# Linear attention and a routed mixture of experts on one core: seven raw and eleven split weight buffers instead of eleven and nine, splits six steps ahead instead of five, and small table columns kept in PSUM

## The chip, the cores and the metric

The kernel runs on one core of a Trainium2 chip. The metric is the device time of one execution in microseconds (us). Before the change it is 616.91 us (median of 3 runs, 615.19 to 617.08).

A core has five engines that run their own instruction streams in order and meet through semaphores: TensorE (PE, matmuls; its weight loads are listed as PEld), VectorE (DVE), ScalarE (ACT), GpSimd (POOL) and SyncE (SP, which issues most DMAs). SBUF is the large on-chip memory, PSUM the small one that matmuls write.

## The reference

```python
# attention: 8 batches, 8 heads, 576 rows, head size 64, 128 features
proj = einsum('bhsd,df->bhsf', x, w_phi)
proj = proj - max(abs(proj), axis=-1)
phi  = concatenate([exp(proj), exp(-proj)])
kv   = einsum('bhsf,bhsd->bhfd', phi(k), v);  z = sum(phi(k), axis=2)
attn = einsum('bhsf,bhfd->bhsd', phi(q), kv) / (phi(q) . z + 1e-6)

# experts: x is attn as (4608 rows, 512); 8 experts, hidden size 1024
do_compute = x @ w_skip > 0
e_idx  = argmax(x @ w_gate, axis=1);  gate_w = softmax(x @ w_gate) at e_idx
y      = gate_w * (relu(x @ w1[e_idx]) @ w2[e_idx])
out    = x + y where do_compute, else x
```

A row goes through one expert, the one with the highest gate, and rows with a skip score of zero or less go through none. All results are float32.

## The kernel before

**Two stages.** The first 337 us compute the attention, batch by batch, and the gate of each row; rows go to a table in DRAM (`xrows`) and to the output. The second stage runs the experts, and the change touches this stage alone.

**Expert slots and steps.** The rows of an expert are gathered into slots of 256 rows (kinds E and D), 192 rows (C) or 128 rows (S). The slots run in a fixed order, E E E C C (S with C) C (D with S) C D, numbered by kind: E0, E1, E2, C0, C1, S0, C2, C3, D0, S1, C4, D1. The weights of a slot are read in eight chunks of 512 KB, four of `w1` and four of `w2`. One chunk is one **step**; there are 96, numbered k = 0 to 95. E0 has steps 0 to 7, E1 8 to 15, E2 16 to 23, C0 24 to 31, C1 32 to 39. S0 and C2 share 40 to 55: S0's `w1` 40 to 43, half of C2's `w1` 44 and 45, S0's `w2` 46 to 49, the rest of C2's `w1` 50 and 51, C2's `w2` 52 to 55.

**What a step needs.** `fetch` (line 175) issues the load of chunk k on SP's queue into a raw buffer `wraw_c` (lines 184 and 187): *load k*. `split` (line 190) makes two tensors of it for matmuls at fp32 accuracy: ACT copies the chunk, rounded, to `hi` (line 195), then DVE (one instruction of 1024 columns) or POOL (four of 256 columns) subtracts it from the raw one to give `lo` (line 200): *split k*. Both halves lie in one of the pair buffers `w`. PE multiplies by `hi` and `lo`: `mm1` (lines 919, 922, 932, 933, 935) and `mm2` (946 to 951) for E, C and D, `half1` (848 to 850) and `half2` (869 to 871) for S.

**Buffers.** From chunk 12 on there are eleven raw buffers and nine pair buffers. A raw buffer is free for load k + 11 when split k is done; a pair buffer is free when PE is through step k.

**The order.** From line 1177 on, the order on each engine is the order in the code. A planner (lines 1144 to 1151) makes a time `T[k]` for each step and `parted[k]` for each split, from fixed costs. At the start of step k the loop (line 1203) emits the splits of up to five steps ahead, as far as the planner thinks that they can be done by then, and with split k also load k + 11. Then come PE's matmuls of step k, then extra work that is due at this step: gathers of rows (line 213, DMAs that POOL issues), the transposes `x` of gathered rows (lines 806 to 810), the stores of a finished slot (DVE `o` and `si`, lines 893 to 905, then a scatter that POOL issues, line 879), and pieces of `tables`.

**The tables.** `tables` (line 966) runs on DVE during steps 5 to 20. It works out from the counts of rows which rows go to which slot: per 128-row tile and expert it makes `tm`, reduces it to columns of 36 values (`pe`, `cc`, line 1029 and 1034), combines these in short instructions (`rk`, `lt`, `col`, lines 1030 to 1041), and compares `col` with a row of numbers (`eq`, line 1061) for PE, which sums up the indices in PSUM bank K.

Of the kernel before, what the change touches and what calls it, by code (L numbers as in the profile page):

```python
# [18 lines left out]
P = 128  # L19
# [5 lines left out]
def kernel(  # L25
# [23 lines left out]
    NT = NTOK // P  # L49
# [67 lines left out]
    eid0 = const.tile([1, 3], I32, name="eid0")  # L117
    idg0 = const.tile([P, 3, 2], I32, name="idg0")
    pad0 = const.tile([P, 3, 2], I32, name="pad0")
    const.tile([1, 40], I32, name="spare")  # L120
    mark = const.tile([1, 32], I32, name="mark")[:, 0:1]

    ft = const.tile([P, NSL, 4], I32, name="ft")
# [51 lines left out]
    def fetch(which, wap, c):  # L175
        i = nchunk[0]

        j = i % 4 if i < 12 else (i - 8) % 11
        rawp = wpool[0 if j < 4 else 3]
        nchunk[0] += 1  # L180
        raw = rawp.tile([P, 1024], F32, tag="wraw%d" % j, name="wraw_c", bufs=1)
        if which == 1:
            src = wap[:, :, c * FC:(c + 1) * FC].rearrange("o (k p) f -> p (o k) f", p=P)
            nc.sync.dma_start(out=raw.rearrange("p (k f) -> p k f", f=FC), in_=src)
        else:
            src = wap[:, c * FC:(c + 1) * FC, :].rearrange("o (k p) m -> p (o k) m", p=P)
            nc.sync.dma_start(out=raw.rearrange("p (k m) -> p k m", m=DM), in_=src)
        return which, i, raw

    def split(chunk, eng):  # L190
        which, i, raw = chunk
        s = i % 9
        pair = wpool[1 if s < 4 else 2].tile([P, 2, 1024], F32R, tag="w%d" % s, name="w", bufs=1)
        hi, lo = pair[:, 0], pair[:, 1]
        nc.scalar.activation(out=hi, in_=raw, func=AF.Copy)  # L195

        n = 256 if eng is nc.gpsimd else 1024
        for a in range(0, 1024, n):
            r = slice(a, a + n)
            eng.tensor_tensor(out=lo[:, r], in0=raw[:, r], in1=hi[:, r].bitcast(F32), op=ALU.subtract)  # L200
        w = FC if which == 1 else DM
        return hi.rearrange("p (k f) -> p k f", f=w), lo.rearrange("p (k f) -> p k f", f=w)
# [761 lines left out]
    start = {"E": 0, "D": 0, "C": NSD, "S": NS2}  # L964

    def tables():
        cn = bank("K")[:, 0:E]
        nc.tensor.matmul(cn, ones_b, Stot, start=True, stop=True)
        yield
        ni = const.tile([P, E], I32, name="ni")  # L970
# [40 lines left out]
        nc.vector.tensor_tensor(out=cf[:, 2], in0=cf[:, 2], in1=cf[:, 1], op=ALU.subtract)  # L1011

        rk = const.tile([P, NT], F32, name="rk")
        pe = const.tile([P, NT], F32, name="pe")
        tm = const.tile([P, NT, E], F32, name="tm")
        cc = const.tile([P, 3, NT], F32, name="cc")
        col = const.tile([P, NT], F32, name="col")
        lt = const.tile([P, NT], F32, name="lt")
        pk = const.tile([P, E], F32, name="pk")

# [8 lines left out]
        nc.vector.tensor_reduce(out=pe, in_=tm, axis=AX.X, op=ALU.add)  # L1029
        nc.vector.scalar_tensor_tensor(out=rk, in0=pe, scalar=-2.0, in1=RKH, op0=ALU.mult, op1=ALU.add)  # L1030
        yield
        for c in range(3):
            nc.vector.tensor_tensor(out=tm, in0=OH, in1=per_e(cf[:, c], NT), op=ALU.mult)
            nc.vector.tensor_reduce(out=cc[:, c], in_=tm, axis=AX.X, op=ALU.add)
        yield
        nc.vector.tensor_tensor(out=lt, in0=rk, in1=cc[:, 1], op=ALU.is_lt)
        nc.vector.tensor_tensor(out=col, in0=cc[:, 0], in1=cc[:, 2], op=ALU.subtract)
        nc.vector.tensor_tensor(out=col, in0=col, in1=lt, op=ALU.mult)
# [153 lines left out]
    with tc.manual_schedule():  # L1192
# [4 lines left out]
        for k, (w, x, c) in enumerate(steps):  # L1197
# [96 lines left out]
```

## Time and profile before

| | before |
|---|---|
| median of 3 runs | 616.91 us |
| profiled execution | 617.51 us |
| its span, first to last instruction | 615.8 us |
| mean granted TensorE clock | 0.984 |
| PE busy over the span | 571.6 us (93%) |
| DVE / ACT / POOL busy | 509.9 / 331.0 / 381.5 us |
| loads of weight chunks | 96 of 512 KB, 5.2 us median from issue to landing |

The time of an execution is its span and some 1.7 us around it. A row of the profile names the line, the engine, the operation and the tiles as out<-in. In the view in order of time (the timeline) a row begins with its start and its duration in us, several instructions of one kind in a row are one row with a count, and the bracket at its end is the engine's idle time ahead of it and who ended it. The list of waits sums such idle times up: total us, how many, the longest. The table by stretches gives each engine's busy time with its count of instructions, the granted clock as a share of full speed, the DMA engines' busy share and GB/s.

### The profile page before, as it was taken

The numbers are of one execution on the slowest core, as the hardware profiler recorded it, in microseconds if no ns is written. First come the engines' busy times: TensorE is split into PE (matmuls) and PEld (weight loads), VectorE is DVE, ScalarE is ACT, GpSimd is POOL, SyncE is SP. The second block draws the span as 40 slices with busy tenths as digits, with TensorE's granted clock in tenths as the row PEclk, the third lists the DMA queues.
The fourth block names the chain that finished last, engine by engine and source line by source line (L and its number), as shares of the span: only waits on it lengthen the run. The fifth ranks groups of instructions, "written<-read, shape, count | busy, mean of one in ns | idle before, by whom it ended". The sixth has DMA issues, their size and how long they took to land. (4 is left out here: it accounts for less than half of the span.)

```text
span 615.8 us, 18780 instructions
## 1 busy us (share of the span) xinstructions
PE 571.6 (93%) x7486; PEld 467.4 (76%) x7486; DVE 509.9 (83%) x1081; ACT 331.0 (54%) x649; POOL 381.5 (62%) x415
## 2 busy tenths in 40 slices
PE   4899999999999999998899799789999799999993
PEld 2577777767777677776667789588889589989892
DVE  5899999999989999999997679967688877956851
ACT  3465556556655555655544454334658556666620
POOL 5665585494855967667754756855467983559121
PEclk9899999999999999999999899999999899999997
DMA  9998888987677766423153499577686599597200
GB/s 157 160 157 150 186 184 178 196 184 142 134 162 160 160 114 155 119 73 113 37 160 127 136 338 341 170 275 228 216 263 203 178 297 327 175 318 238 76 19 30
DMA packets 250234, 108.34 MB, mean 176 GB/s; under 512 B 192417, under 2 KB 235553, under 8 KB 250144
## 3 DMA queue, kind: packets, MB, share of 16 engines
q1 hardware_dynamic: 245632, 97.58, 60.7%
q0 software_dynamic: 3200, 9.45, 4.5%
q8 instruction: 60, 0.98, 0.7%
q10 hardware_dynamic: 1312, 0.08, 0.1%
q14 instruction: 30, 0.25, 0.1%
HBM read 83.86 MB, written 24.02 MB: 175 GB/s over the span
## 5 line engine op out<-in xcount | busy, mean ns | idle before, releaser
L200 POOL TENSOR_TENSOR w<-wraw_c,w 128x256 fp32r<-128x256 f32 x124 | 109.8, 920 | 42.1 <-ACT w L195 36.0
L380 POOL TENSOR_TENSOR z<-ek 128x512 f32<-128x512 f32 x64 | 81.2, 1273 | 77.0 <-ACT ek L373 54.1
L195 ACT ACTIVATE w<-wraw_c 128x1024 fp32r<-128x1024 f32 x96 | 97.6, 1052 | 3.8 <-DMA wraw_c<-in_moe_w_dram 3.5
L200 DVE TENSOR_TENSOR w<-wraw_c,w 128x1024 fp32r<-128x1024 f32 x65 | 87.8, 1359 | 13.9 <-ACT w L195 12.8
L354 DVE TENSOR_REDUCE m<-ps_P 128x8 f32<-128x1024 f32 (+2 forms) x86 | 88.6, 1030 | 7.1 <-PE ps_P L347 7.1
L357 DVE TENSOR_TENSOR u<-ps_P,m 128x1024 f32<-128x1024 f32 (+2 forms) x86 | 88.8, 1033 | 2.9
L347 PE MATMUL ps_P<-wsrc,xT 64*64 64x128 f32 x2048 | 79.3, 283 | 11.7 <-DMA raw<-in_k_dram 7.1
L513 PEld LDWEIGHTS ps_O<-kva,eq 128*64 128x64 f32 x2048 | 74.0, 136 | 16.3 <-issue 5.8
L513 PE MATMUL ps_O<-kva,eq 128*64 128x74 f32 x2048 | 77.4, 228 | 3.8 <-DVE lgm L476 3.7
L347 PEld LDWEIGHTS ps_P<-wsrc,xT 64*64 64x64 f32 x2048 | 57.4, 135 | 28.2 <-issue 20.3
L399 ACT ACTIVATE eq<-ps_U 128x512 f32<-128x512 f32 x64 | 37.9, 593 | 64.7 <-PE ps_U L393 64.2
L415 PE MATMUL ps_K<-ek,v 128*64 128x256 f32 x512 | 72.0, 400 | 0.0
L879 POOL DMA_INDIRECT out_dram<-o,si x22 | 28.8, 1309 | 66.8 <-DVE si L878 60.4
L946 PE MATMUL ps_O<-w,hh 128*128 128x512 f32 x160 | 64.1, 401 | 0.0
L633 POOL TENSOR_SCALAR OP<-iota_p,rkp,wcol 128x128 bf16<-128x128 f32 x62 | 48.4, 790 | 24.0 <-DVE RKH L636 17.8
L372 ACT ACTIVATE ek<-u 128x512 f32<-128x512 f32 x64 | 40.5, 633 | 38.7 <-DVE u L357 22.8
L950 PE MATMUL ps_O<-w,hh 128*128 128x512 f32 x120 | 47.8, 398 | 3.5 <-DVE w L200 2.9
L393 PE MATMUL ps_U<-ident,u 128*128 128x128 f32 x288 | 48.9, 287 | 1.0 <-DVE u L357 0.6
L324 DVE STREAM_TRANSPOSE xT<-raw 128x512 f32<-128x512 f32 x64 | 44.7, 701 | 5.9 <-PE ps_P L347 2.6
L415 PEld LDWEIGHTS ps_K<-ek,v 128*64 128x64 f32 x512 | 32.1, 138 | 21.5 <-issue 11.3
L951 PE MATMUL ps_O<-w,hlo 128*128 128x512 f32 x120 | 47.6, 397 | 0.1
L384 POOL TENSOR_TENSOR z<-z 128x512 f32<-128x512 f32 x32 | 40.8, 1274 | 2.5
(253 smaller groups left out, 1214.1 us busy)
## 6 DMA issues: line engine op xcount, KB each, us to landing
wraw_c<-in_moe_w_dram SPq DMA_DIRECT2D x96, 512.0 KB, 5.2
raw<-in_k_dram SPq DMA_DIRECT2D x64, 144.0 KB, 3.1
raw<-in_q_dram SPq DMA_DIRECT2D x64, 144.0 KB, 4.1
v<-in_v_dram SPq DMA_DIRECT2D x64, 128.0 KB, 2.8
out_dram<-xm SPq DMA_DIRECT2D x16, 512.0 KB, 4.2
xrows<-xm SPq DMA_DIRECT2D x8, 516.0 KB, 4.1
xrows<-xm SPq DMA_DIRECT2D x8, 512.0 KB, 4.4
vt<-in_v_dram SPq DMA_DIRECT2D x32, 32.0 KB, 2.6
```

What stands on the lines that cost most here:

```text
L195: nc.scalar.activation(out=hi, in_=raw, func=AF.Copy)
L200: eng.tensor_tensor(out=lo[:, r], in0=raw[:, r], in1=hi[:, r].bitcast(F32), op=ALU.subtract)
L347: nc.tensor.matmul(p[s * 64:s * 64 + 64, hd, (nj + j) * NF:(nj + j + 1) * NF], xT[r, g * P + s * 64:g * P + s * 64 + 64], wsrc[r], start=T ...
L354: nc.vector.tensor_reduce(out=m.rearrange("p (j h) -> p j h", h=2), in_=pv, axis=AX.X, op=ALU.max, apply_absolute_value=True)
L357: nc.vector.tensor_tensor(out=uu[:, 0:2 * nj, :].rearrange("p (j h) f -> p j h f", h=2), in0=pv, in1=m.rearrange("p (j h o) -> p j h o", h ...
L380: zeng.tensor_tensor(out=z, in0=e[:, 0:2, :], in1=e[:, 2:4, :], op=ALU.add)
L393: nc.tensor.transpose(t[:, tt * P:(tt + 1) * P], uu[:, tt, :], ident)
L415: nc.tensor.matmul(o[hd * 64:hd * 64 + 64, :], u.v[:, 2 * hd + pr, g * D:(g + 1) * D], u.e[i][:, 2 * j + hd, :], start=(g == 0), stop=False,)
L513: nc.tensor.matmul(ov[s * 64:s * 64 + 64, 2 * j + hd, :], e[:, half, j, hd, s * 64:s * 64 + 64], kva[:, half, 2 * pr + hd, :], start=(half ...
L633: (nc.vector if last else nc.gpsimd).tensor_scalar(out=OP[:, t0 + t, c, :], in0=iota_p, scalar1=rkp[:, t:t + 1], scalar2=wcol[:, NT:NT + 1 ...
L946: nc.tensor.matmul(y[sub], hh[:, t], wh[:, fi, :], start=first, stop=False)
L950: nc.tensor.matmul(y[sub], hh[:, t], wl[:, fi, :], start=False, stop=False)
```

## The change

Three things are changed together. There are seven raw buffers instead of eleven from chunk 12 on, so load k + 7 goes with split k instead of load k + 11, and eleven pair buffers instead of nine. Splits are emitted up to six steps ahead instead of five. And four of the tables' columns (`pe`, `col`, and two of the three of `cc`, now `c0` and `c1`) lie in PSUM bank K, behind the counts and the indices, so that one tile of that bank is held from the first to the last piece of `tables`; `c2`, `rk` and `lt` stay in SBUF. The planner's formulas follow the new numbers.

```diff
-        j = i % 4 if i < 12 else (i - 8) % 11
+        j = i % 4 if i < 12 else (i - 8) % 7
...
-        s = i % 9
+        s = i % 11
...
-        cn = bank("K")[:, 0:E]
+        kb = bank("K")
+        cn = kb[:, 0:E]
...
-        pe = const.tile([P, NT], F32, name="pe")
+        ix = kb[:, E:E + NCOL]
+        pe, col, c0, c1 = (kb[:, a:a + NT] for a in range(E + NCOL, E + NCOL + 4 * NT, NT))
         tm = const.tile([P, NT, E], F32, name="tm")
-        cc = const.tile([P, 3, NT], F32, name="cc")
-        col = const.tile([P, NT], F32, name="col")
+        c2 = const.tile([P, NT], F32, name="c2")
...
-        nc.vector.tensor_tensor(out=lt, in0=rk, in1=cc[:, 1], op=ALU.is_lt)
-        nc.vector.tensor_tensor(out=col, in0=cc[:, 0], in1=cc[:, 2], op=ALU.subtract)
+        nc.vector.tensor_tensor(out=lt, in0=rk, in1=c1, op=ALU.is_lt)
+        nc.vector.tensor_tensor(out=col, in0=c0, in1=c2, op=ALU.subtract)
...
-        arrive = 0.0 if k < FIRST else max(ready[k - 1] + (3.0 if k < 12 else 2.35), parted[k - (4 if k < 12 else 11)] + 4.0)
+        arrive = 0.0 if k < FIRST else max(ready[k - 1] + (3.0 if k < 12 else 2.35), parted[k - (4 if k < 12 else 7)] + 4.0)
...
-            while nxt < len(steps) and nxt <= k + 5 and (nxt <= k + 1 or parted[nxt] <= T[k] + 1.0):
+            while nxt < len(steps) and nxt <= k + 6 and (nxt <= k + 1 or parted[nxt] <= T[k] + 1.0):
...
-                for n in (range(nxt + 4, nxt + 5) if nxt < 7 else range(11, 19) if nxt == 7 else range(nxt + 11, nxt + 12)):
+                for n in (range(nxt + 4, nxt + 5) if nxt < 7 else range(11, 15) if nxt == 7 else range(nxt + 7, nxt + 8)):
```

The first piece that moves is on ACT, in E2 (`w<-wraw_c` is ACT's half of a split, `x` the transposed rows of E2, `hh` the output of step 16). Splits up to 21 stand where they stood; step 16 now emits two, 21 and 22, and from there on every split is emitted one step earlier than before.

```order
 L809 ACTIVATE x<-ps_U 128x4x128 x2
-L195 ACTIVATE w<-wraw_c 128x1024 x2
+L195 ACTIVATE w<-wraw_c 128x1024 x3
 L824 ACTIVATE hh<-ps_P 128x512
 L195 ACTIVATE w<-wraw_c 128x1024
```

One ACT split more stands ahead of `hh` of step 16; behind it the rows read as before, but each split is that of the next chunk.

On DVE, at the piece of `tables` in step 8, the column `pe` becomes a part of the tile `ps_K`; `rk` is the first instruction that reads it.

```order
-L1025 TENSOR_TENSOR pk<-pks 128x8
-L1026 TENSOR_TENSOR pk<-pk,pks 128x8
-L1028 TENSOR_TENSOR tm<-OH,pk 128x216
-L1028 TENSOR_TENSOR tm<-OH,pks 128x72
-L1029 TENSOR_REDUCE pe<-tm 128x36
-L1030 SCALAR_TENSOR_TENSOR rk<-pe,RKH 128x36
+L1026 TENSOR_TENSOR pk<-pks 128x8
+L1027 TENSOR_TENSOR pk<-pk,pks 128x8
+L1029 TENSOR_TENSOR tm<-OH,pk 128x216
+L1029 TENSOR_TENSOR tm<-OH,pks 128x72
+L1030 TENSOR_REDUCE ps_K<-tm 128x36
+L1031 SCALAR_TENSOR_TENSOR rk<-ps_K,RKH 128x36
```

The order is the same; `rk` had two inputs in SBUF and now has one there and one in PSUM.

On POOL, in the steps that S0 and C2 share, `w` are quarter splits (four to a chunk), `out_dram` the scatter of a finished sub-slot, `mark` a marker behind it and `xg` a gather of rows. Before:

```order
L200 TENSOR_TENSOR w<-wraw_c,w 128x256 x8
L879 DMA out_dram<-o,si 4608x512
L888 MEMSET mark 1x1
L879 DMA out_dram<-o,si 4608x512
L888 MEMSET mark 1x1
L200 TENSOR_TENSOR w<-wraw_c,w 128x256 x4
L213 DMA xg<-xrows,ft 128x514
L213 DMA xg<-xrows,ft 64x514
L200 TENSOR_TENSOR w<-wraw_c,w 128x256 x12
```

and with the change:

```order
L200 TENSOR_TENSOR w<-wraw_c,w 128x256 x12
L879 DMA out_dram<-o,si 4608x512
L888 MEMSET mark 1x1
L879 DMA out_dram<-o,si 4608x512
L888 MEMSET mark 1x1
L200 TENSOR_TENSOR w<-wraw_c,w 128x256 x4
L213 DMA xg<-xrows,ft 128x514
L213 DMA xg<-xrows,ft 64x514
L200 TENSOR_TENSOR w<-wraw_c,w 128x256 x8
```

Split 45 moves ahead of C1's two scatters and split 47 ahead of C3's gathers; 49 and 51 follow these.

More of the change, by code (lines that the diff above doesn't have):

```diff
@@ L119 @@
     pad0 = const.tile([P, 3, 2], I32, name="pad0")
-    const.tile([1, 40], I32, name="spare")
+    const.tile([1, 64], I32, name="spare")
     mark = const.tile([1, 32], I32, name="mark")[:, 0:1]
@@ L1031, in tables @@
         yield
-        for c in range(3):
+        for c, cc in enumerate((c0, c1, c2)):
             nc.vector.tensor_tensor(out=tm, in0=OH, in1=per_e(cf[:, c], NT), op=ALU.mult)
-            nc.vector.tensor_reduce(out=cc[:, c], in_=tm, axis=AX.X, op=ALU.add)
+            nc.vector.tensor_reduce(out=cc, in_=tm, axis=AX.X, op=ALU.add)
         yield
-        nc.vector.tensor_tensor(out=lt, in0=rk, in1=cc[:, 1], op=ALU.is_lt)
-        nc.vector.tensor_tensor(out=col, in0=cc[:, 0], in1=cc[:, 2], op=ALU.subtract)
+        nc.vector.tensor_tensor(out=lt, in0=rk, in1=c1, op=ALU.is_lt)
+        nc.vector.tensor_tensor(out=col, in0=c0, in1=c2, op=ALU.subtract)
         nc.vector.tensor_tensor(out=col, in0=col, in1=lt, op=ALU.mult)
-        nc.vector.tensor_tensor(out=col, in0=col, in1=cc[:, 2], op=ALU.add)
+        nc.vector.tensor_tensor(out=col, in0=col, in1=c2, op=ALU.add)
         nc.vector.tensor_tensor(out=col, in0=col, in1=rk, op=ALU.add)
         nc.vector.scalar_tensor_tensor(out=col, in0=rk, scalar=0.0, in1=col, op0=ALU.is_ge, op1=ALU.mult)
-        ix = bank("K")[:, 0:NCOL]
         C = 9
@@ L1146 @@
     for k, (w, x, c) in enumerate(steps):
-        arrive = 0.0 if k < FIRST else max(ready[k - 1] + (3.0 if k < 12 else 2.35), parted[k - (4 if k < 12 else 11)] + 4.0)
+        arrive = 0.0 if k < FIRST else max(ready[k - 1] + (3.0 if k < 12 else 2.35), parted[k - (4 if k < 12 else 7)] + 4.0)
         ready.append(arrive)
-        parted.append(max(arrive, T[k - 9] + 3.0 if k >= 9 else 0.0, parted[k - 1] + 1.25 if k else 0.0))
+        parted.append(max(arrive, T[k - 11] + 3.0 if k >= 11 else 0.0, parted[k - 1] + 1.25 if k else 0.0))
         T.append(max(T[k - 1] + took[steps[k - 1][1][0]] + (1.0 if w == 1 and c == 0 else 0.0) if k else 2.0,
```

## The prediction

> **What bounds the kernel now.** First the table by stretches, for PE, DVE, POOL and the granted clock (columns: busy us and instructions of PE, PEld, DVE, ACT, POOL; clock; DMA share; GB/s).
>
> ```profile
> span 615.8 us, 18780 instructions
> core 0: us, PE busy (x) PEld busy (x) DVE busy (x) ACT busy (x) POOL busy (x), PEclk, DMA share, GB/s
> 376.00:406.00 30.00, 24.18 (x133) 19.82 (x132) 29.17 (x39) 10.49 (x14) 22.36 (x27) 0.94 0.71 238
> 406.00:470.00 64.00, 63.01 (x436) 56.86 (x435) 46.67 (x84) 36.52 (x59) 38.71 (x44) 1.00 0.69 224
> 470.00:497.00 27.00, 23.47 (x141) 20.49 (x140) 22.86 (x30) 16.77 (x28) 25.81 (x28) 0.94 0.67 221
> 497.00:592.00 95.00, 93.85 (x583) 85.01 (x582) 72.74 (x106) 58.05 (x89) 51.67 (x57) 1.00 0.66 223
> ```
>
> PE is the bound of the expert stage, but for two places: in 376 to 406 (the end of E1, the start of E2) DVE is busy for 29.17 of 30 us and PE idles 5.8; in 470 to 497 (S0 with C2) POOL is busy for 25.81 of 27 and PE idles 3.5. In both the clock falls. Elsewhere only PE's own work is left, which the change doesn't touch. The list of PE's waits from 330 us on says what ended the idle time:
>
> ```profile
> PE ps_O L870 <- POOL w L200: 3.2, 3, 1.4
> PE ps_O L950 <- DVE w L200: 2.9, 1, 2.9
> PE ps_P L919 <- DVE hsum L925: 2.1, 4, 1.0
> PE ps_P L933 <- DVE x L810: 1.7, 1, 1.7
> PE ps_O L950 <- POOL w L200: 0.6, 1, 0.6
> PE ps_P L935 <- POOL w L200: 0.5, 2, 0.3
> PE ps_P L922 <- POOL w L200: 0.3, 1, 0.3
> ```
>
> These are 2.9 + 1.7 + 0.6 + 0.5 = 5.7 us in the first place, 3.2 + 0.3 = 3.5 in the second, and 2.1 of single waits for `hsum`. Behind each place's gaps the clock is at a half for 3.4 us:
>
> ```profile
> 397.60:401.00 3.40, 3.40 (x10) 2.61 (x9) 3.40 (x4) 0.00 (x0) 0.74 (x1) 0.50 0.60 170
> 486.40:489.80 3.40, 3.40 (x10) 2.63 (x9) 3.40 (x3) 1.52 (x2) 3.40 (x3) 0.50 0.82 261
> 396.57 0.50 PE L950 MATMUL ps_O<-w,hh 128*128 128x512 f32 x1 [2.92 <-DVE w L200]
> 403.12 0.38 PE L933 MATMUL ps_P<-x,w 128*128 128x256 f32 x1 [1.68 <-DVE x L810]
> ```
>
> Half a clock for 3.4 us costs 1.7 us of PE's work, twice. All of it together, 5.7 + 3.5 + 2.1 + 3.4 = 14.7 us, is the most that the change can win.
>
> **Part 1, the columns in PSUM.** Why DVE is late at the first place is read from its timeline, beside POOL's:
>
> ```profile
> 378.48 5.57 POOL L200 TENSOR_TENSOR w<-wraw_c,w 128x256 fp32r<-128x256 f32 x8
> 378.54 5.57 DVE L1030 SCALAR_TENSOR_TENSOR rk<-pe,RKH 128x36 f32<-128x36 f32 x1
> 384.03 1.21 DVE L200 TENSOR_TENSOR w<-wraw_c,w 128x1024 fp32r<-128x1024 f32 x1
> 386.74 1.10 DVE L1033 TENSOR_TENSOR tm<-OH,cf 128x288 f32<-128x288 bf16 x1
> 387.41 10.93 POOL L200 TENSOR_TENSOR w<-wraw_c,w 128x256 fp32r<-128x256 f32 x12
> 388.36 0.46 DVE L1033 TENSOR_TENSOR tm<-OH,cf 128x288 f32<-128x288 bf16 x1
> 390.07 0.77 DVE L1037 TENSOR_TENSOR col<-cc 128x36 f32<-128x36 f32 x1
> 390.88 0.66 DVE L1038 TENSOR_TENSOR col<-col,lt 128x36 f32<-128x36 f32 x1
> 393.66 1.19 DVE L1061 TENSOR_TENSOR eq<-i,col 128x558 bf16<-128x558 f32 x1
> 394.77 1.75 DVE L200 TENSOR_TENSOR w<-wraw_c,w 128x1024 fp32r<-128x1024 f32 x1
> 397.04 0.72 DVE L1061 TENSOR_TENSOR eq<-i,col 128x558 bf16<-128x558 f32 x1
> ```
>
> `rk`, 36 values wide, takes 5.57 us: it begins just behind the first of eight POOL instructions (splits 11 and 12) and ends when the eighth does. The five short `col` instructions take 0.77 and 0.66 (four alike), each as long as one POOL quarter split beside it. What they share is two inputs in SBUF. A reading from PSUM was not held up beside POOL anywhere; the nearest row of such a size is this one:
>
> ```profile
> 362.47 0.19 DVE L627 TENSOR_TENSOR rm<-ps_K,OH 128x40 f32<-128x40 f32 x1
> ```
>
> With `pe`, `col`, `c0`, `c1` in PSUM, `rk` and the five `col` instructions have one SBUF input each. At 0.19 each they save 5.57 - 0.19 = 5.4 and 0.77 + 4 x 0.66 - 5 x 0.19 = 2.5; the first `eq` saves 1.19 - 0.72 = 0.5: 8.4 us of DVE. No row shows a write of DVE to PSUM; its bounds are 0.19 and the 0.66 that the SBUF form takes beside POOL, which for the eight writes (`pe`, `c0`, `c1`, five of `col`) is at most 3.8 us given back; I take 0.19, the row with an operand in that bank. The Trainium skill (SBUF — State Buffer, Who interferes with whom) says that a DVE instruction with two SBUF inputs and a GpSimd one that reads SBUF exclude each other for a whole instruction, and that one SBUF input doesn't contend; the `col` rows agree (one quarter split, 0.7 us), the row of `rk` doesn't: it lost eight in a row. By that page alone `rk` would lose one turn, and this part would save 0.7 + 2.5 + 0.5 = 3.7 us of DVE, not 8.4.
>
> Some of it comes back. Split 13 on DVE (384.03) now stands at 378.8, beside POOL's run: 1.75 instead of 1.21, as in the row at 394.77. The `tm` products keep two SBUF inputs: 1.10 instead of 0.46 for the two that did not meet POOL before. That is 0.5 + 1.3, and DVE is 6.6 us earlier at the transposes of E2's rows, 396.5 instead of 403.1.
>
> What is late next: POOL. DVE's split and three products go between POOL's quarter splits and hold them up by what DVE takes, 1.2 + 3 x 0.46 = 2.6 at most. Behind them wait two gathers and split 14, which PE waits for already (the 0.6). So PE gains 2.9 + 1.7 + 1.7 (clock) = 6.3, less 0 to 2.6: between 3.7 and 6.3. I take **-5.0**.
>
> **Part 2, splits one step earlier.** From step 16 on each split stands one PE step (1.45 to 2.85 us by the planner's `took`) earlier on ACT, DVE and POOL. What it costs: one split more on DVE and ACT ahead of step 16's output, 1.21 and 1.05 us; PE does steps 17 to 19 on other banks meanwhile and its next reader of that output is step 20, three steps on, so nothing. Eleven pairs hold the seven steps in flight with four over, so no split waits for PE. What it wins is at S0 with C2, on POOL:
>
> ```profile
> 464.79 7.59 POOL L200 TENSOR_TENSOR w<-wraw_c,w 128x256 fp32r<-128x256 f32 x8 [6.66 <-ACT w L195]
> 475.91 3.89 POOL L200 TENSOR_TENSOR w<-wraw_c,w 128x256 fp32r<-128x256 f32 x4
> 482.90 12.66 POOL L200 TENSOR_TENSOR w<-wraw_c,w 128x256 fp32r<-128x256 f32 x12
> 460.37 1.04 ACT L195 ACTIVATE w<-wraw_c 128x1024 fp32r<-128x1024 f32 x1
> 478.28 0.95 PE L919 MATMUL ps_P<-x,w 128*128 128x384 f32 x4
> ```
>
> The rows are POOL's splits 41 and 43, then 45, then 47, 49 and 51, ACT's half of split 40, and PE's start of step 45. Between POOL's rows lie C1's scatters (3.5 us from 472.4) and C3's gathers (3.1 us from 479.8). POOL had stood idle for 6.66 us, for ACT's half of split 41. That half takes the place of split 40's now (460.37), so POOL begins at 461.5, 3.3 us earlier. At 3.8 us a split, split 45 ends at 472.9; behind the scatters 47 ends at 480.2, ahead of where it began before (482.90); behind the gathers 49 ends at 487.1 and 51 at 490.9. PE, from 478.3 on at 2.3 us a step of C2 and 1.4 of S0, is at step 47 at 482.0, at the second half of 49 at 485.7, where it waits 1.4, and at the last quarter of 51 at 491.3. So 1.4 of the 3.5 us stay, and 486.4 to 489.8 runs at full clock: 3.5 + 1.7 - 1.4, **-3.8**, with bounds of -2 (the clock falls all the same) and -5.2.
>
> The waits for `hsum` stand where DVE's stores meet POOL's splits. POOL's are earlier now and leave DVE's stores alone; of 2.1 us I take **-0.5**, between 0 and -2.1.
>
> **Part 3, seven raw buffers.** Load k now waits for split k - 7 instead of k - 11.
>
> ```profile
> SPq L187 <- POOL w L200: 46.2, 15, 7.0
> L200 DVE TENSOR_TENSOR w<-wraw_c,w x65: 1204/1225/2531, 342.1 to 590.8; 128x1024 fp32r<-128x1024 f32 x65
> DMA to landing us min/median/max: 3.4/5.5/10.3
> 483.09 4.83 ACT L195 ACTIVATE w<-wraw_c 128x1024 fp32r<-128x1024 f32 x5
> 493.74 0.33 ACT L924 ACTIVATE hsum<-ps_P 128x192 f32<-128x192 f32 x1 [5.82 <-PE ps_P L922]
> ```
>
> SP waits for freed buffers already (46.2 us for POOL's splits in front of `w2` loads alone), so loads go out when a split ends. (The second row is for the first rival below: ns, the shortest, median and longest DVE split.) SP's read of the tables' `ovf` now stands ahead of loads 34 and 35; DVE writes it in step 20 and these loads wait for splits of steps 21 and 22, so nothing. A chunk then has seven steps less its own split: 7 x 2.4 = 17 us in C, some 13 in S0 with C2. It lands in 5.5 (median) to 10.3 (longest). The cover is 3 us at the least. The tightest place is again S0 with C2: load 56 waits for split 49, until 487.1, and lands at 492.6, and ACT's copy, which stands ahead of `hsum` of step 50, holds ACT up. In that place ACT had 5.82 us of idle time, PE needs step 50's output only in step 54, some 497, and DVE has it by 496.5. So 0, but with 1 us of cover; the other end is 3 us lost.
>
> **The sum.** -5.0 - 3.8 - 0.5 = -9.3 us against the profiled execution's 617.5 (its span of 615.8 and 1.7 around it): 608.2. That execution lies 0.6 above the median of the runs shown, so the median comes to **607.6 us**.
>
> **Rivals.**
>
> - *The lockout passes on* (chance 0.16). Split 13, next behind `rk` and with two SBUF inputs, is kept out until POOL's run ends at 384.05, as `rk` was. For: nothing in the profile says why `rk` lost eight turns. Against: in every other row split 13's kind lost a turn or two (the longest DVE split is 2.53 us). DVE then saves only 2.5 + 0.5 = 3.0 at E2's transposes, the term is -3.0, and the time 609.6.
> - *The clock drops stay* (0.08): the half-clock stretches hang on something else than these gaps, and 3.4 us are not won, 611.0. Against: both stretches begin within 1.1 us of a gap's end. The Trainium skill (TensorE: Matmul & The Clock Gate, Part 1) has the clock fall after an idle window of some 3.4 us. By that page gaps of 2.92, and of 1.36 with 0.69, would be too short to be the cause; the trace has the stretches right behind them.
> - *A late raw chunk takes back part 2* (0.12). ACT's copy of chunk 56 or its neighbours waits longer than ACT's idle time: 3 us back, 610.6.
> - *Everything goes* (0.08): POOL is not held up, all gaps fall: 602.2 to 604.
> - *Slower: seven buffers don't feed the splits* (0.06). In the place of the waits removed, each loop of seven steps takes landing, copy and split instead of seven steps of PE. It decides where landing passes 17 - 1 - 1.2 = 14.8 us; at 16 us each of (96 - 22) / 7 = 10 loops loses 1.2 and the gain of 9.3 is gone, at 17 us the time is 607.6 + 22 = 630. Against: the longest landing was 10.3 with eleven buffers, and fewer loads in flight don't make one longer.
> - *It doesn't do what it says* (0.06): the waits only change their names, PE still stands for POOL in both places, and the time is within 0.3%, about what a measurement of this kernel can tell from no change.
>
> My forecast has the remaining 0.44. **The range**: the lower end takes the bounds of parts 1 and 2, -6.3 - 5.2 - 1.5 = -13.0, 604.0; the upper end takes in the lockout, the clock and the late chunk, 611.5. That leaves out some 0.18. **Faster** by over 0.3% (below 615.1): 0.88; within: 0.06; slower: 0.06.
>
> **What would show it.** `rk` at 0.2 us and the `col` instructions under 0.3; no DVE row above 2 us beside POOL's run for splits 11 and 12; PE's wait for split 15 gone and that for split 14 up to 2 us; POOL's splits 41, 43, 45 in one run from 461.5 less part 1's gain; no clock of 0.5 behind 350 us. It would be wrong if ACT waits for DMAs by more than some us, if a DVE write to PSUM takes 0.6, or if `hsum` ends new gaps of PE in C2 and C4.

## The result, and the profile after

| | before | with the change |
|---|---|---|
| median, first comparison | 617.00 us (4 runs, 615.19 to 621.04) | 609.67 us (4 runs, 609.24 to 610.28) |
| ratio, 95% interval | | 0.9881 [0.9854, 0.9908] |
| median, once more (e0) | 614.76 us (24 runs) | 610.00 us (7 runs) |
| ratio, 95% interval | | 0.9921 [0.9889, 0.9953] |
| profiled execution, its span | 617.51, 615.8 us | 609.66, 607.9 us |

The change is faster by 7.3 us in the first comparison and by 4.8 us in the second; the intervals overlap. One of the 24 runs (623.04 us) and one of the twelve of b0 below (622.55) were slow and don't count in the ratios. The forecast was 607.6 us, in a range of 604.0 to 611.5. The table by stretches of the profile after (columns as before):

```profile
core 0: us, PE busy (x) PEld busy (x) DVE busy (x) ACT busy (x) POOL busy (x), PEclk, DMA share, GB/s
376.00:406.00 30.00, 27.43 (x211) 24.25 (x210) 23.34 (x42) 11.80 (x15) 26.98 (x33) 0.89 0.65 228
406.00:470.00 64.00, 63.74 (x390) 57.53 (x389) 48.89 (x86) 39.67 (x64) 42.15 (x47) 1.00 0.72 236
470.00:497.00 27.00, 24.57 (x138) 21.46 (x137) 21.95 (x30) 17.12 (x29) 19.16 (x24) 1.00 0.82 276
497.00:592.00 95.00, 92.71 (x583) 84.30 (x582) 67.61 (x100) 53.02 (x81) 50.34 (x52) 1.00 0.62 208
```

In 376 to 406 DVE fell from 29.17 to 23.34 us (by 5.8 us; the forecast had DVE 6.6 us earlier at the end of the place), and POOL rose from 22.36 to 26.98: the load changed sides. PE is busier by 3.25 us there, but the clock went down, from 0.94 to 0.89. In 470 to 497 the clock is full and POOL is no longer the busiest engine. In 497 to 592 PE is busy for 1.1 us less. The list of PE's waits from 330 us on names what is left (total us, times, longest):

```profile
PE ps_P L919 <- DVE hsum L925: 2.5, 4, 1.2
PE ps_O L946 <- DVE o L893: 2.4, 1, 2.4
PE ps_P L935 <- POOL w L200: 2.2, 3, 1.1
```

The waits for `x` at 403 us, for split 15 and for splits 49 and 51 are gone. The wait for split 11 (L935) grew from 0.5 to 2.2, and a wait for `o` of 2.4 is new. The first place in order of time, POOL, DVE and PE together, and the clock behind it:

```profile
374.83 1.09 POOL L879 DMA_INDIRECT out_dram<-o,si  x1 [5.02 <-DVE si L878]
377.25 7.50 POOL L200 TENSOR_TENSOR w<-wraw_c,w 128x256 fp32r<-128x256 f32 x8
377.31 0.20 DVE L1031 SCALAR_TENSOR_TENSOR rk<-ps_K,RKH 128x36 f32<-128x36 f32 x1
377.42 1.73 DVE L200 TENSOR_TENSOR w<-wraw_c,w 128x1024 fp32r<-128x1024 f32 x1
379.79 0.39 PE L935 MATMUL ps_P<-x,w 128*128 128x256 f32 x1 [1.11 <-POOL w L200]
380.76 0.44 PE L935 MATMUL ps_P<-x,w 128*128 128x256 f32 x1 [0.58 <-POOL w L200]
381.74 0.58 PE L935 MATMUL ps_P<-x,w 128*128 128x256 f32 x1 [0.54 <-POOL w L200]
384.03 0.20 DVE L1041 TENSOR_TENSOR ps_K<-ps_K,rk 128x36 f32<-128x36 f32 x1
384.50 0.74 DVE L1061 TENSOR_TENSOR eq<-i,ps_K 128x558 bf16<-128x558 f32 x1
```

The table by stretches of the same profile, for the half-clock stretch behind PE's gaps:

```profile
380.90:387.70 6.80, 6.26 (x22) 5.32 (x23) 6.49 (x16) 2.78 (x4) 6.31 (x8) 0.50 0.49 157
```

`rk` takes 0.20 us and the `col` instructions 0.20, and DVE runs on while POOL works. But POOL's eight quarter splits (11 and 12) take 7.50 us where they took 5.57, and PE, which begins step 11 at 377.4 and needs its `lo` from 378.4 on, waits for them quarter by quarter. From the second of these gaps on the clock is at a half for 6.8 us, which costs 3.4. In the profile before PE's waits for the same quarters were these:

```profile
380.68 0.38 PE L935 MATMUL ps_P<-x,w 128*128 128x256 f32 x1 [0.24 <-POOL w L200]
381.36 0.39 PE L935 MATMUL ps_P<-x,w 128*128 128x256 f32 x1 [0.29 <-POOL w L200]
```

The last quarter of split 11 came 2.9 us after the start of POOL's run there (378.48 to 381.36), and 4.5 us after it with the change (377.25 to 381.74).

The second place, S0 with C2:

```profile
455.86 3.14 POOL L200 TENSOR_TENSOR w<-wraw_c,w 128x256 fp32r<-128x256 f32 x4 [4.64 <-ACT w L195]
459.18 9.07 POOL L200 TENSOR_TENSOR w<-wraw_c,w 128x256 fp32r<-128x256 f32 x8 [0.18 <-ACT w L195]
476.98 5.60 POOL L200 TENSOR_TENSOR w<-wraw_c,w 128x256 fp32r<-128x256 f32 x8
477.98 4.89 DVE L836 SCALAR_TENSOR_TENSOR hlo<-hsum,hh 128x256 fp32r<-128x256 f32 x1 [0.59 <-ACT hh L834]
482.99 4.62 DVE L200 TENSOR_TENSOR w<-wraw_c,w 128x1024 fp32r<-128x1024 f32 x4
487.54 0.74 DVE L893 SCALAR_TENSOR_TENSOR o<-ps_O,xg 128x512 f32<-128x512 f32 x1
488.33 0.50 PE L946 MATMUL ps_O<-w,hh 128*128 128x512 f32 x1 [2.43 <-DVE o L893]
503.89 0.97 PE L919 MATMUL ps_P<-x,w 128*128 128x384 f32 x4 [1.23 <-DVE hsum L925]
507.19 0.97 PE L919 MATMUL ps_P<-x,w 128*128 128x384 f32 x4 [0.75 <-DVE hsum L925]
```

POOL starts split 41 at 455.86, and 41, 43 and 45 run almost without a break, as forecast; 49 and 51 are done at 482.6 and PE no longer stands for them. But an instruction of DVE, `hlo` of line 836, begins beside POOL's run and is held for 4.89 us (its shortest is 0.4); four splits and then `o` stand behind it, and PE waits for `o`.

### The profile page after: what moved, and what is told of

It is laid out like the page before. It is cut to its first block, busy times and chain, and to the rows that moved or that the text cites. A ratio compares the mean times of both kernels' runs of the same rounds, so it can differ in the third digit from the quotient of the medians.

```text
span 607.9 us, 18782 instructions
## 1 busy us (share of the span) xinstructions
PE 567.2 (93%) x7486; PEld 465.9 (77%) x7486; DVE 500.4 (82%) x1081; ACT 330.7 (54%) x649; POOL 382.5 (63%) x415
## 5 line engine op out<-in xcount | busy, mean ns | idle before, releaser
L380 POOL TENSOR_TENSOR z<-ek 128x512 f32<-128x512 f32 x64 | 81.2, 1273 | 76.7 <-ACT ek L373 54.2
L200 DVE TENSOR_TENSOR w<-wraw_c,w 128x1024 fp32r<-128x1024 f32 x65 | 85.8, 1331 | 12.6 <-ACT w L195 10.9
L347 PEld LDWEIGHTS ps_P<-wsrc,xT 64*64 64x64 f32 x2048 | 57.4, 135 | 27.9 <-issue 19.1
L879 POOL DMA_INDIRECT out_dram<-o,si x22 | 28.8, 1310 | 55.9 <-DVE si L878 49.4
```

Source lines behind the costliest of these rows:

```text
L347: nc.tensor.matmul(p[s * 64:s * 64 + 64, hd, (nj + j) * NF:(nj + j + 1) * NF], xT[r, g * P + s * 64:g * P + s * 64 + 64], wsrc[r], start=T ...
L380: zeng.tensor_tensor(out=z, in0=e[:, 0:2, :], in1=e[:, 2:4, :], op=ALU.add)
```

## The experiments

Each kernel ran beside the kernel before on one chip, in three batches (e1 to e4; e0, e5, e8, e9; b0, e6, e11, e12), and its ratio is against the runs of its batch, whose median for the kernel before was 614.49, 614.76 and 615.85 us. "Stage" below is the time from PE's start of step 0 to the end of the span, read from the profiled execution; what lies ahead of it, the attention stage, has the same instructions in all of them and took 342.7 to 348.6 us in these executions.

| kernel | median us (runs) | ratio, 95% interval | stage | steps 0 to 20 | 20 to 40 | 40 to 53 | 53 to end |
|---|---|---|---|---|---|---|---|
| before, first profile | 616.91 (3) | | 272.7 | 73.7 | 51.6 | 30.9 | 116.5 |
| b0, before again | 616.77 (12) | 1.0010 [0.9987, 1.0034] | 276.6 | 76.5 | 51.6 | 29.2 | 119.3 |
| e1, columns alone | 615.55 (12) | 1.0017 [0.9996, 1.0038] | 269.0 | 68.9 | 51.6 | 29.2 | 119.3 |
| e3, columns and buffers | 614.95 (12) | 1.0001 [0.9982, 1.0020] | 269.0 | 69.6 | 51.6 | 29.4 | 118.4 |
| e6, look-ahead alone | 611.08 (6) | 0.9919 [0.9895, 0.9943] | 264.9 | 67.9 | 51.6 | 27.3 | 118.1 |
| e2, columns and look-ahead | 609.92 (6) | 0.9925 [0.9899, 0.9950] | 265.0 | 68.8 | 50.6 | 27.3 | 118.3 |
| the change, first profile | 609.67 (4) | 0.9881 [0.9854, 0.9908] | 265.0 | 69.2 | 50.6 | 27.3 | 117.9 |
| e0, the change again | 610.00 (7) | 0.9921 [0.9889, 0.9953] | 264.5 | 68.7 | 50.6 | 27.3 | 117.9 |
| e8, pe in SBUF | 610.69 (6) | 0.9920 [0.9889, 0.9951] | 266.1 | 70.2 | 50.6 | 27.9 | 117.2 |
| e5, split 11 on DVE | 611.44 (12) | 0.9931 [0.9903, 0.9959] | 266.6 | 71.0 | 50.6 | 28.6 | 116.3 |
| e9, hlo in two | 611.99 (12) | 0.9961 [0.9938, 0.9984] | 266.4 | 68.8 | 50.8 | 29.9 | 116.8 |
| e4, pe in SBUF, tiles shifted | 615.00 (10) | 1.0014 [0.9997, 1.0032] | 264.9 | 68.9 | 50.7 | 28.5 | 116.8 |
| e11, split 11 ahead | 609.52 (6) | 0.9895 [0.9872, 0.9917] | 264.0 | 67.0 | 51.6 | 28.7 | 116.7 |
| e12, and split 49 on DVE | 608.32 (6) | 0.9877 [0.9855, 0.9899] | 264.0 | 67.1 | 51.6 | 27.2 | 118.2 |

### The three parts apart: e1, e2, e3, e6

All start from the change but e6, which starts from the kernel before. e1 has the columns alone:

```diff
-        j = i % 4 if i < 12 else (i - 8) % 7
+        j = i % 4 if i < 12 else (i - 8) % 11
-        s = i % 11
+        s = i % 9
-            while nxt < len(steps) and nxt <= k + 6 and ...
+            while nxt < len(steps) and nxt <= k + 5 and ...
```

with the planner's and the loads' numbers put back too. e2 has the first two of these edits, e3 the last alone. e6 is the kernel before with one edit:

```diff
-            while nxt < len(steps) and nxt <= k + 5 and ...
+            while nxt < len(steps) and nxt <= k + 6 and ...
```

> The tables' columns in PSUM, with eleven raw buffers, nine pairs and splits five steps ahead as before. If the columns and the six steps win in separate places, this has the first alone: rk at 0.2 us, PE about 3 us earlier behind the tables' place, the waits for POOL at S0 with C2 (3.5 us before) still there: 612.5 to 614.5 us. If the whole gain hangs on the buffers and the order, 616 to 617.5.

> The change with eleven raw and nine pair buffers kept; splits six steps ahead and columns in PSUM as in the change. The order on PE, DVE, ACT and POOL is that of the change, only loads go out earlier. If the exchange of buffers is neutral: 609 to 610.5 us, as the change. If seven raw buffers cost the time that ACT waits for chunks (7.1 us in the change, 3.5 before): 606.5 to 608.5, ACT's wait back at some 3.5. If fewer loads in flight help the gathers: 611 or more.

> The change with splits five steps ahead; seven raw and eleven pair buffers, columns in PSUM. If the order of the splits alone wins at S0 with C2: as columns alone, 612.5 to 614.5 us, with 3 to 4 us of PE waits for POOL between 465 and 500. If the buffers win there: 609 to 610.5.

> The kernel before with the look-ahead of six alone: columns in SBUF, eleven raw buffers and nine split ones. Theory A (nearly all of the change's gain is the look-ahead): within 1.5 us of the change, ratio 0.991 to 0.995. Rival B (the columns in PSUM are worth the 3 to 5 us that the prediction gave them): the change plus 3 to 5 us, ratio 0.998 to 1.002, with rk held for 4 us or more and the wait for x L810 (1.7 us at 403 in before) still there.

With a look-ahead of five nothing is won that the runs can tell, with the columns (e1) or with columns and buffers (e3): the theory that the columns are worth several us by themselves fails here. With six the time falls by 4.6 to 4.8 us, with the columns (e2) or without (e6). The buffers make no difference in either pair. So the gain is the look-ahead's, and what the columns add to it can't be told from zero (the intervals are some 1.5 us to either side). The profiles show a good part of it from step 40 on: from there to the end (the last two columns together) the four with five ahead take 147.4 to 148.5 us, nine with six ahead 144.9 to 145.6, and e9, with its added operations, 146.7. In the trace of e6 `rk`, with both inputs in SBUF, met POOL's run and lost a single turn; and PE waited for split 11 as in the change (timeline):

```profile
379.20 7.52 POOL L200 TENSOR_TENSOR w<-wraw_c,w 128x256 fp32r<-128x256 f32 x8
379.27 0.83 DVE L1030 SCALAR_TENSOR_TENSOR rk<-pe,RKH 128x36 f32<-128x36 f32 x1
382.45 0.38 PE L935 MATMUL ps_P<-x,w 128*128 128x256 f32 x1 [1.32 <-POOL w L200]
383.42 0.58 PE L935 MATMUL ps_P<-x,w 128*128 128x256 f32 x1 [0.58 <-POOL w L200]
```

The look-ahead can't be why `rk` was let in. The first split that it moves is 22, in step 16; up to step 15 e6 has the instructions of the kernel before, in the same order. So the 5.57 us are not fixed by the order of the program: the kernel before lost them in both of its profiles (the second follows below), and e6 did not. PE's steps 0 to 15 took 58.1 and 61.6 us in those two and 54.2 in e6, which is no longer than the 55.0 to 55.9 of the change, e0, e1, e2 and e3 with their columns in PSUM. Where `rk` is not held, the columns win nothing there that these profiles show.

e1 shows what stands in the place of the hold. In its trace, too, `rk` takes 0.20 us, POOL's run for 11 and 12 takes 7.46, and PE waits for split 11 four times; a half-clock stretch of 6.8 us begins behind the third wait. At S0 with C2 `hlo` is held for the whole of a run of twelve (timeline of e1):

```profile
381.34 0.38 PE L935 MATMUL ps_P<-x,w 128*128 128x256 f32 x1 [0.48 <-POOL w L200]
382.30 0.39 PE L935 MATMUL ps_P<-x,w 128*128 128x256 f32 x1 [0.57 <-POOL w L200]
383.29 0.58 PE L935 MATMUL ps_P<-x,w 128*128 128x256 f32 x1 [0.60 <-POOL w L200]
384.28 0.58 PE L935 MATMUL ps_P<-x,w 128*128 128x256 f32 x1 [0.41 <-POOL w L200]
480.52 8.30 DVE L836 SCALAR_TENSOR_TENSOR hlo<-hsum,hh 128x256 fp32r<-128x256 f32 x1 [0.59 <-ACT hh L834]
```

### The kernel before once more: b0

> The kernel before once more, profiled. Part 1 of the prediction took the 5.57 us of rk from one execution. With pe in SBUF rk took 0.37 us in run e4 and 0.83 in e8, so it may be chance. Theory A (what POOL's run does to rk is fixed by the program): rk takes 5 to 6 us again, PE's waits at 396 and 403 us are 2.9 and 1.7 again. Theory B (it differs from execution to execution): rk takes under 2 us in this one, and the span lies 2 to 4 us under the 615.8 of the first. The chip's 614.5 to 614.8 against the 616.9 of the first three runs speaks a little for B.

`rk` was held again, for 5.61 us, and one of the `tm` products behind it for 8.26, by a run of twelve (timeline of b0):

```profile
378.30 5.60 POOL L200 TENSOR_TENSOR w<-wraw_c,w 128x256 fp32r<-128x256 f32 x8
378.35 5.61 DVE L1030 SCALAR_TENSOR_TENSOR rk<-pe,RKH 128x36 f32<-128x36 f32 x1
387.27 8.23 POOL L200 TENSOR_TENSOR w<-wraw_c,w 128x256 fp32r<-128x256 f32 x12
387.57 8.26 DVE L1033 TENSOR_TENSOR tm<-OH,cf 128x288 f32<-128x288 bf16 x1
396.96 0.79 PE L951 MATMUL ps_O<-w,hlo 128*128 128x512 f32 x1 [7.70 <-DVE hlo L825]
486.11 8.31 DVE L836 SCALAR_TENSOR_TENSOR hlo<-hsum,hh 128x256 fp32r<-128x256 f32 x1 [0.59 <-ACT hh L834]
```

Theory A held for `rk`; the rest of the expectation (the same waits of PE) did not. In the first profile that `tm` product took 0.46, `hlo` 2.17, and PE's longest wait at the place was 2.92; here it is 7.70. This execution took 621.5 us, 4.7 above its own median. So a profile of the kernel before is one draw among several, and both draws lie above the median. With e6 this speaks for a shorter loss at the table place in the usual execution than either profile shows, and would explain why e1 is 3.7 us shorter in its profiled stage than the first profile of before and no shorter in its median. How often an execution is held was not shown: executions without a profile don't show their waits. Besides, the whole span of e1's execution is only 1.6 us shorter than the first of before (614.2 against 615.8): ahead of step 0 it took 345.2 us instead of 343.1, with the clock at a half for 10.2 us there instead of 3.4.

### The first column back in SBUF: e4 and e8

> The change with the one column pe back in SBUF, so that rk has two SBUF inputs again beside POOL's splits 11 and 12; all else as the change. If two SBUF inputs behind a POOL run are what kept rk out: rk takes 2 us or more, DVE is later by that at E2's rows, and the time is 611 to 614 us. If the 5.57 us were a single event: rk takes 0.9 us or less and the time is 609 to 610.5.

> The change with its first column (pe) back in SBUF, and the spare tile cut by what pe takes, so that every other tile lies where it does in the change. Run e4 moved every tile behind the constants by 160 bytes, to an odd multiple of 32, and its loads of raw<-in_k_dram took 4.3 us instead of 3.2, its attention stage 348.6 us instead of 342.9. Theory A (that start of the tiles is what cost e4 its 5 us, and rk is not held by POOL's run once the splits come a step earlier): within 1 us of the control, attention stage 343 to 345 us, rk under 2 us. Theory B (rk is held again by POOL's subtractions, as in before): rk 3 to 6 us, the control plus 1.5 to 4 us.

```diff
-    const.tile([1, 64], I32, name="spare")
+    const.tile([1, 24], I32, name="spare")
...
-        pe, col, c0, c1 = (kb[:, a:a + NT] for a in range(E + NCOL, E + NCOL + 4 * NT, NT))
+        col, c0, c1 = (kb[:, a:a + NT] for a in range(E + NCOL, E + NCOL + 3 * NT, NT))
+        pe = const.tile([P, NT], F32, name="pe")
```

e4 lacks the first of the two edits. It took 615.00 us (614.23 to 616.49), all of the change's gain lost. Its stage was no longer than the change's, 264.9 us; its attention stage was, 348.6. The 160 bytes that `pe` takes, an odd multiple of 32, had shifted the tiles of both stages behind the constants, the loads' targets among them. The loads of `k` in the first 100 us from the view of DMA issues (queue, count, KB each, median us to landing), of e4 and then of e8:

```profile
raw<-in_k_dram SPq DMA_DIRECT2D x32, 144.0 KB, 4.3
```
```profile
raw<-in_k_dram SPq DMA_DIRECT2D x36, 144.0 KB, 3.3
```

And the first 50 us by stretches, of e4 and then of e8 (the last three columns are clock, DMA share and GB/s):

```profile
0.00:50.00 50.00, 33.08 (x510) 22.88 (x513) 33.10 (x58) 21.18 (x46) 27.19 (x52) 0.97 1.16 143
```
```profile
0.00:50.00 50.00, 36.02 (x609) 25.71 (x610) 37.68 (x67) 24.81 (x54) 31.07 (x55) 1.00 0.90 155
```

With the addresses kept e8 is within a microsecond of the change (610.69 against 610.00), its attention stage took 344.1 us, and `rk`, its inputs in SBUF, took 0.83. Theory A held for the time and the cause of e4's loss. Its reason for `rk` does not follow: splits 11 and 12 come no earlier with six ahead, so e8 is, like e6, an execution in which `rk` was not held. (e4 says nothing of it: `rk` took 0.37 there, but it began ahead of POOL's run.) e4 also shows what a line of the change may be worth that the diff further up leaves out and the prediction passed over: the spare tile goes from 40 to 64 words. Counted with each tile rounded up to 32 bytes, as `pe` is (36 values of 4 bytes in 160), the tiles behind the constants then move by 512 bytes; with 40 words they would have moved by 608, an odd multiple of 32 like e4's 160. The change without this line was not run.

### Where the gain at the table place went: e5 and e11

> The change with split 11 on DVE and split 13 on POOL. In the change PE waits three times for POOL's split 11 (1.11 + 0.58 + 0.54 us at 379.8 to 381.7) and then runs at half clock for 6.83 us. Theory A (that is where part of the columns' gain went): the three gaps go, no half clock begins between 376 and 386 us, and the time is 2 to 5 us under the control. Rival B (one DVE split more ahead of the column operations makes them late, or split 13 is late on POOL now): a new wait of 1 to 3 us for x L810 or for split 13 at 386 to 400 us, time within 1 us of the control. Rival C: the half clock comes from the gap in any of these places; if a gap over 1 us is left anywhere in 376 to 406 us, at least 1.7 us of the gain stay out.

```diff
-'gp': (0, 1, 2, 4, 6, 8, 9, 11, 12, 14, 17, 19, 21)
+'gp': (0, 1, 2, 4, 6, 8, 9, 12, 13, 14, 17, 19, 21)
```

In the trace the gaps for split 11 went, and two for split 14 came at 391 and 395 us (2.31 and 1.06 us), with 6.8 us at half clock behind the first: rival B and C. The median is 1.4 us above the control's, and the intervals overlap. The wait moved from split 11 to split 14: it seems to go with POOL's work there as a whole, not with split 11 alone.

> The change with one thing moved: POOL's split 11 stands ahead of the two scatters of rows that wait on POOL for DVE's si, not behind them. PE, DVE and ACT keep their order. In the control POOL lay idle for 5.91 us ahead of the scatter at 375.8, though chunk 11 had been copied by ACT at 368.2, and started split 11 at 378.2, while PE wanted it at 378.9. Theory A (that is where the columns' gain went): split 11 runs at 370 to 373 us, PE's gaps of 0.56 + 0.58 + 0.60 us at 381 to 383 and those of 0.51 + 0.69 for split 14 go, and with them a half-clock stretch of 3.4 to 6.8 us wherever they had set one off: 3 to 5 us under the control's 610.0. Rival B (the order only moves the wait to split 14 or to x L810): 0 to 1.5 us under it.

```diff
-            for f in [f for s, f in before if s == k]:
-                f()
-            while nxt < len(steps) and nxt <= k + 6 and ...
...
+            for first in (True, False):
+                while nxt < len(steps) and nxt <= k + 6 and ...
...
+                    if first and (v or nxt != 11):
+                        break
...
+                if first:
+                    for f in [f for s, f in before if s == k]:
+                        f()
```

POOL and PE at the table place of e11:

```profile
370.93 2.94 POOL L200 TENSOR_TENSOR w<-wraw_c,w 128x256 fp32r<-128x256 f32 x4 [0.61 <-ACT w L195]
379.78 1.09 POOL L879 DMA_INDIRECT out_dram<-o,si  x1 [5.91 <-DVE si L878]
382.20 4.45 POOL L200 TENSOR_TENSOR w<-wraw_c,w 128x256 fp32r<-128x256 f32 x4
386.70 0.50 PE L950 MATMUL ps_O<-w,hh 128*128 128x512 f32 x1 [0.29 <-POOL w L200]
393.13 0.50 PE L950 MATMUL ps_O<-w,hh 128*128 128x512 f32 x1 [0.65 <-POOL w L200]
```

Split 11 runs in what was POOL's idle time ahead of the scatter. Of 2.9 us of PE's waits for splits 11 and 14 in the control 0.9 is left (for 12 and 14), and steps 0 to 20 are 1.7 us shorter (67.0 against 68.7). No half-clock stretch begins there, but none did in the control's profile either. The median is 0.5 us under the control's of the other batch, the ratio 0.0026 lower, some 1.6 us; the two intervals overlap. That is between A and B: the cause of these waits was named rightly, their price (3 to 5 us) was not.

### What holds DVE beside POOL's run: e9 and e12

> The change with the first operation of line 836 (max with 0, then minus hh, in one SCALAR_TENSOR_TENSOR with both sources in SBUF) written as two: a TENSOR_SCALAR max in place and a TENSOR_TENSOR subtraction. All 20 of them. Theory A (what POOL's run holds for 5 to 8 us is the form SCALAR_TENSOR_TENSOR; a TENSOR_TENSOR loses one turn of 0.5 to 1 us): beside POOL's splits 49 and 51 the subtraction takes at most 1.5 us instead of 4.89, PE's wait of 2.43 us for o at 488 us goes, and the time is 1 to 3 us under the control, the 20 added operations of 0.2 to 0.3 us notwithstanding. Rival B (any DVE operation of this shape with two SBUF sources that meets POOL's unbroken run is held to its end): one of them takes 4 to 5 us again, and the time is the control's or up to 1 us more.

```diff
-            (nc.gpsimd if (CFG["cp"] >> (a == P)) & 1 else nc.vector).scalar_tensor_tensor(
+            if a == 0:
+                nc.vector.tensor_scalar(out=hv[:, :, a:b], in0=hv[:, :, a:b], scalar1=0.0, scalar2=None, op0=ALU.max)
+                nc.vector.tensor_tensor(out=o, in0=hv[:, :, a:b], in1=hh[:, :, a:b].bitcast(F32), op=ALU.subtract)
+                continue
+            nc.vector.scalar_tensor_tensor(
```

(`cp` is 0, so the instruction ran on DVE before as well.) DVE of e9 in order of time, beside POOL's run for 49 and 51, which lasts from 478.91 to 484.48 us:

```profile
478.73 5.91 DVE L837 TENSOR_SCALAR hsum<-hsum 128x256 f32<-128x256 f32 x1 [0.59 <-ACT hh L834]
484.68 0.42 DVE L838 TENSOR_TENSOR hlo<-hsum,hh 128x256 fp32r<-128x256 f32 x1
```

Neither theory held as written. The TENSOR_SCALAR, the first to meet the run, was held for it, and the subtraction behind it was free. PE waited 2.75 us for `o` instead of the control's 2.39, and the median is 2.0 us above the control's (the intervals overlap). With the `tm` product of b0 that makes three forms that were held through a whole run. My theory that the form decides is refuted.

> The kernel of e11 with two splits exchanged besides: 49 goes to DVE and 53 to POOL. Beside L836's first operation at 478 us POOL's unbroken run is then four pieces and not eight, and one DVE split of 1.2 us fewer stands ahead of o. Theory A (the 2.4 us wait for o at 488 us is that operation's hold by POOL's run, plus the four splits behind it): the hold is at most 3 us, the wait for o falls by 2 us or more, the waits for hsum at 503 and 507 us (1.23 + 0.76) change by less than 1 us, and the time is 1.5 to 3 us under e11. Rival B (split 53 on POOL comes late for PE, or the hold lasts as long as POOL finds work): a new wait of 1 to 2 us for split 53, time within 1 us of e11.

```diff
-                        (x_[0] == "C" and w_ == 1 or x_[0] == "S") and c_ % 2 == 1)
+                        (x_[0] == "C" and w_ == 1 or x_[0] == "S") and c_ % 2 == 1 and nxt != 49 or nxt == 53)
```

POOL, DVE and PE of e12 in order of time:

```profile
476.59 5.59 POOL L200 TENSOR_TENSOR w<-wraw_c,w 128x256 fp32r<-128x256 f32 x8
476.89 5.58 DVE L836 SCALAR_TENSOR_TENSOR hlo<-hsum,hh 128x256 fp32r<-128x256 f32 x1 [0.59 <-ACT hh L834]
486.80 0.50 PE L946 MATMUL ps_O<-w,hh 128*128 128x512 f32 x1 [2.20 <-DVE o L893]
```

Split 53 was ready when 51 ended, so the run was again eight pieces long and the hold 5.58 us: here it lasted as long as POOL found work, the second half of rival B. The wait for `o` fell only from 2.46 to 2.20. e12 has the lowest median of the study, 608.32 us, 1.2 under e11 beside it, but their intervals overlap and their profiled stages are equally long (264.0 us). The 2.0 us between the two profiled spans lie ahead of step 0, where the kernels are the same. So a gain from this edit is not shown.

### The control: e0

> The change itself once more, as the control for the other runs of this call. If its time against the kernel before is a property of the two programs, the ratio is 0.985 to 0.991 again. If the 609.7 was helped by a lucky position of the half-clock stretches in its profiled run (none behind the 1.41 + 1.62 us gaps at 343 to 345 us, none in the first 30 us), the median is 1 to 3 us nearer to before, ratio 0.991 to 0.995, near the 0.9925 of the kernel with the old buffers and six ahead.

The ratio of 0.9921 is what the expectation gave for a first result helped by chance; the two intervals overlap. Its trace has the same three places of loss: split 11 (0.56 + 0.58 + 0.60 us, with 0.51 + 0.69 for split 14 behind it), `o` (2.39), `hsum` (1.23 + 0.76).

## Why the prediction was right, and where it wasn't

**The time.** Forecast 607.6 against 609.67 in the first comparison, -9.3 us against -7.3 (and -4.8 in the second). Seen in the two profiled executions the difference of 7.9 us in span is 0.2 ahead of step 0, 4.5 in steps 0 to 20, 1.0 in 20 to 40, 3.6 in 40 to 53, less 1.4 after. Chance is in the 4.5, both ways: the profile before has 3.4 us at half clock from 346.4 us on, behind gaps of 1.4 and 1.6 us that both profiles have, and the profile after has none there; its own 6.8 us at 380.9 are missing in e0. That the time fell into the range is luck in part: the larger term of the sum, part 1, can't be told from zero in the medians (e1), and the look-ahead, forecast at 3.8, brought 4.6 to 4.8.

**Part 1, -5.0.** The step on DVE was right but for the `tm` products (0.46 us each, two were forecast at 1.10): `rk` 0.20, `col` 0.20, the first `eq` 0.74, split 13 1.73 (forecast 1.75), no wait for `x`. Two steps failed. "What is late next" put the delay of POOL at 2.6 us at most (it was 7.50 - 5.57 = 1.9) on two gathers and split 14; but split 11, at the head of that run, was itself due. While DVE was held POOL had the run to itself. In the two profiles of the kernel before, `rk` is held and PE waits 0.5 and 0.3 us for split 11. In the nine profiles with split 11 in this place in which it isn't, the wait is 2.2 (the change), 1.7 (e0), 2.1 (e1), 1.2 (e2), 1.7 (e3), 2.0 (e4), 1.9 (e6), 1.7 (e8) and 2.3 (e9). Each turn that DVE won POOL lost, and PE needed POOL's first. The second failed step is the premise. The 5.57 us of `rk`, read from one execution, was counted as the columns' to win in every one. e6, with the same order up to step 15 and its columns in SBUF, lost one turn instead of eight, and its steps 0 to 20 are as short (67.9 us) as those of e1 with the columns in PSUM (68.9). With one turn lost the columns save 0.7 + 2.5 + 0.5 = 3.7 us of DVE instead of 8.4. The prediction notes that nothing in the profile says why `rk` lost eight, and counts the eight all the same.

**Part 2, -3.8.** The look-ahead does win at S0 with C2, as forecast, and POOL's run began at 455.86, where the forecast has it (461.5 less the 5.6 us by which step 40 is earlier). Steps 40 to 53 became 3.6 us shorter against the first profile, but 1.9 against b0, and the full clock is not the change's doing: with five ahead b0, e1 and e3 have no half-clock stretch there either, and of the ten profiles with six ahead five have one of 3.4 us at 489 to 494 us, behind the wait for `o` (e4, e5, e8, e9, e11). Counted from step 40 to the end the gain is 2.2 us against the first profile and 3.3 against b0. The forecast remainder of 1.4 for split 49 did not come, and 2.43 for `o` came in its place: the hold of `hlo`, for which the first profile was the exception (timeline of before):

```profile
483.22 2.17 DVE L836 SCALAR_TENSOR_TENSOR hlo<-hsum,hh 128x256 fp32r<-128x256 f32 x1 [0.59 <-ACT hh L834]
```

In the thirteen others the instruction that first reads `hsum` there takes 4.2 to 8.3 us.

**hsum, -0.5.** Between steps 20 and 40 a microsecond went (50.6 against 51.6), and behind step 53, where the first profile of before lacks the two waits of 1.23 and 0.75 us, 1.4 came back: +0.4 in all. But b0 and e1 have these two waits as well (1.30 and 0.76 in b0), and PE's waits for `hsum` sum up to 4.0 us in each of them against 2.5 in the change. So the sign of this term depends on which profile of before is taken.

**Part 3, 0.** Right: e2 and e0 have the same ratio to within 0.0004, e1 and e3 to within 0.0016. The sign that the prediction named did come, ACT's waits for weight chunks rose from 3.5 to 7.1 us in the profiles; in e2, with eleven raw buffers, they are 1.5, and e2 is no faster. So they cost nothing that the runs can tell.

**The rivals.** Split 13 was not held. The clock rival was half right: the stretch at 486 went, and that at 398 went too, but twice its length came at 380.9 behind gaps of 1.11 and 0.58 us. The Trainium skill (TensorE: Matmul & The Clock Gate, Part 1) has a free-running window of 3.4 us; the half-clock stretches in all traces are 3.4 or 6.8 us long, but for the one that runs to the end of each, which agrees, but this one follows gaps of a third of the window and less, and after the same 1.41 + 1.62 us at 343 us one profile of the change shows none and the other shows one.

**Open.** What decides whether a DVE instruction that meets POOL's run loses one turn or all of them: `rk` lost eight twice and one turn in e6 and e8 with the same form, starting 0.05 us behind the run's start in b0 and in e8 alike. How often an execution of the kernel before is held. And how the rest of the 4.6 to 4.8 us, beyond the 2 to 3 from step 40 on, is made up.

## What to carry to other kernels

Where two engines exclude each other, freeing one slows the other: before counting the gain, look at which of the two the critical engine needs next. A long wait read from one execution may be that execution's own: profile the kernel before more than once before counting it as a gain, and run each edit alone before adding them up. And when a tile is added or removed ahead of DMA targets, keep their addresses: here 160 bytes cost as much as the whole change won.

## What was not expected of the hardware

- Tiles in SBUF, DMA targets among them, shifted by 160 bytes (only this one shift was tried): loads of 144 KB took 4.3 us to land instead of 3.3, the DMA engines were busy for 1.16 of the time instead of 0.90, at 143 instead of 155 GB/s (e4 and e8).
- A TENSOR_SCALAR in place on SBUF was held through POOL's run (5.91 us, shortest 0.29), as was a TENSOR_TENSOR (8.26 us, shortest 0.44). The Trainium skill (SBUF — State Buffer, Who interferes with whom) says that a TENSOR_TENSOR with both inputs in SBUF contends with GpSimd's reads, that a TENSOR_SCALAR can when it runs in a 2-port mode, and that whoever issues first blocks the other for the whole instruction; the exclusion agrees, but these lost eight and twelve instructions in a row. In which mode the TENSOR_SCALAR ran no trace shows.
- DVE reads and writes PSUM, 36 columns wide, in 0.20 us beside POOL's run (the change), no more than in SBUF without it (`col` of e6, 0.20).
